# Signs of the weights by VectorE, three low bits by ScalarE, fewer TensorE transposes, and other durations in the planner

## The chip, the cores and the metric

The kernel runs on one core of a Trainium2 chip. The metric is device time in microseconds (us) of one execution; each version is timed in several runs and the median counts. One further execution is recorded by the hardware profiler. Engine names in the profile: PE is TensorE (PEld its weight loads), DVE is VectorE, ACT is ScalarE, POOL is GpSimd, SP is SyncE, whose queue (SPq) issues every DMA of this kernel.

## The reference

Clustered attention, followed by a two-layer MLP over its output:

```python
# q, k, v: [4, 8, 768, 64]; centroids: [8, 16, 64]
q_assign = argmax(einsum('bhsd,hcd->bhsc', q_n, c_n))      # rows normalised
k_assign = argmax(einsum('bhsd,hcd->bhsc', k_n, c_n))
scores = where(q_assign == k_assign, q @ k.T / 8, -1e9)
attn = exp(scores - max); attn = attn / (sum + 1e-9)
x = (attn @ v) as [3072, 512]
h = x @ w_in                                               # w_in [512, 2048]
g = s * relu(h) ** 2 + b
out = g @ w_out                                            # w_out [2048, 512]
```

q, k, v and centroids arrive as float32. The two weight matrices arrive as float64, so the kernel has to make float32 of them.

## The kernel before

**Attention.** There are 192 units, one for each batch, block of 128 query rows and head. A unit has its scores on PE (`sc`, two matmul pairs, one with the tiles KA and QA, one with KB and QB), a row maximum on DVE (`ssm<-sc`), an exponential on ACT (`p`), a transpose of `p`, and a product with V on PE (`px`), which DVE scales into `xs`. The first 16 units work in float32: PE transposes `p` (`turned`), ACT copies that out (`PT`), and `px<-vn,PT` is a float32 matmul. The later units split `p` into two float16 halves and let a DMA transpose them. Batch 0 has its K in four pairs of heads (hp 0 to 3: units 0 and 1, 2 and 3, and so on in each block) and its first two query blocks in two halves (hq 0 and 1). K and Q are split, transposed (KA, QA), compared with the centroids (`pk`, `pq`, the one-hot tiles `om`, `oe`, `oo`), and transposed once more with the one-hot part (KB, QB). `turn` does these transposes: with `early` set by PE in pieces of 8 blocks of 128x128, each piece copied out of PSUM by ACT (`KB<-turn`), else by a DMA transpose on SP's queue. Before the change all of batch 0's K and the Q of its first two query blocks are early.

**Weights.** 16 tiles of w_in and 16 of w_out, 128x512 each, are loaded alternately as raw float64 words into `wst` (512 KB each), and narrowed in the order `fetch`, `rebase`, `narrow`, `bound`. `rebase` (ACT) multiplies the high word, taken as float32, by 2^-112 into `w` and takes its sign into `wsg`, of which there are two buffers. `narrow` (DVE) shifts `w` left by three bits, by which the sign drops out, and puts the top three bits of the low word in. `bound` sums the absolute values by a matmul with ones (`pw` with a DVE maximum for w_in, `po`, one accumulating bank, for w_out); then POOL multiplies `w` by the sign. The tile `wst` lies in the pool `slot` of 19 buffers, which also holds the 16 pairs of narrowed weights. The MLP of the first two blocks (`h<-x,w`, `acc<-w,g`) works with these float32 weights; later, weights split into float16 (`ws`) are used.

**Order.** The kernel records each operation as a step; a planner (`Plan.order`) then goes through the steps with an estimated duration for each, gives every engine next what it can start first, and the instructions are emitted in that order. Each engine works through its own list in order. So a changed estimate changes no work, only the order of an engine's list. In the planner, DVE and POOL operations marked as shared push each other back.

Of the kernel before, what the change touches and what calls it, by code (L numbers as in the profile page):

```python
# [37 lines left out]
class Plan:  # L38


    LIGHT = 2.4
    SIGNAL = 40.0

    def __init__(self, tc):
        self.tc = tc
# [83 lines left out]
    def takes(self, step):  # L129

        method, args, kwargs = step.calls[0]
        aps = [a for a in args if isinstance(a, bass.AP)]
        if step.queue.name == "PE":
            total = 0.0
            for _, args, _ in step.calls:
                n = self.width(args[0])
                if args[1].dtype == F32:
                    total += max(n * 4 / self.LIGHT, 112.0)
                else:
                    total += 56.0 if n == P else max(n / self.LIGHT + 2.5, 26.0)  # L140
            return total, False
        n = max(self.width(a) for a in aps)
        banks = any(a.space == PSUM for a in aps)
        small = all(a.dtype in (F16, BF16) for a in aps[:2])
        name = step.queue.name
        if name == "DVE":
            if method in ("tensor_reduce", "reciprocal"):
                return 145 + n / 0.96, method == "reciprocal" and not banks
            if method == "tensor_tensor":
                return 148 + n / 0.96, not banks  # L150
            if method == "scalar_tensor_tensor":
                return (200.0 if n == 1 else 165 + n * 1.1), not banks
            fold = 1 if banks else 4 if small else 2
            return 150 + n / 0.96 / fold, not banks
        if name == "ACT":
            more = 110 if "accum_out" in kwargs else 0
            if banks:
                return (170 + n * 0.84 if small else 140 + n * 1.1 if n > 700 else 130 + n * 0.97) + more, False
            return (100 + n * 1.1 if args[2] == AF.Copy and "scale" in kwargs else 100 + n * 1.0) + more, False
        if method == "tensor_tensor":  # L160
            return 165 + n * 1.93, True
        if method == "tensor_copy":
            return 60 + n * 1.35, True
        return 100.0, True

    def transfer(self, step):
# [6 lines left out]
        n = self.width(ap) // P  # L173
        return (1300.0 if n < 12 else 1480.0), 1300.0, n * 165.0, 500.0

    def order(self):
        steps = self.steps
        after = [[] for _ in steps]
        open_ = [len(s.waits) for s in steps]
        for s in steps:  # L180
# [23 lines left out]
        while left:  # L204
            best = None
            for q, line in pending.items():
                now = clock[q]
                choice = None
                for k in line:
                    at, need = max(ready[k], now), {}  # L210
                    for t in steps[k].tiles:
                        if t.name in held:
                            continue
                        tag = self.tag(t)
                        if turn[t.name] != given[tag] + need.get(tag, 0) or len(spare[tag]) <= need.get(tag, 0):
                            at = None
                            break
                        at = max(at, spare[tag][need.get(tag, 0)])
                        need[tag] = need.get(tag, 0) + 1
                    if at is None:  # L220
                        continue
                    if q == "SP" and len(landed) >= 8:
                        at = max(at, landed[-8])
                    mine = (max(at, now + 30), self.weight[k], at, k)
                    if choice is None or mine < choice:
                        choice = mine
                if choice and (best is None or choice[2] < best[2]):
                    best = choice + (q,)
            _, _, at, k, q = best
            s = steps[k]  # L230
            pending[q].remove(k)
            for t in s.tiles:
                if t.name not in held:
                    held.add(t.name)
                    given[self.tag(t)] += 1
                    spare[self.tag(t)].pop(0)
            started[k] = at
            if q == "SP":
                issue, pre, work, post = self.transfer(s)
                begin = max(at + pre, engines_free)  # L240
                engines_free = begin + work
                clock[q] = at + issue
                end = begin + work + post
                landed.append(end)
            else:
                long, shared = self.takes(s)
                end = at + long
                if q == "DVE" and shared:
                    for a, z in pool[-6:]:
                        if a < at + 60 < z:  # L250
                            end = max(end, z + long - 118)
                    port.append((at + 60, end))
                if q == "POOL":
                    a = at
                    for x, z in port[-6:]:
                        if x < at + 60 < z:
                            a = max(a, z - 60)
                    end = a + long
                    pool.append((a, end))
                clock[q] = end - {"PE": 0, "DVE": 70, "POOL": 45, "ACT": 90}[q]  # L260
                end += 60 if q == "PE" else 0
            for j in after[k]:
                open_[j] -= 1
                same = steps[j].queue.name == q == "PE"
                ready[j] = max(ready[j], end - 60 if same else end + self.SIGNAL)
                if not open_[j]:
                    pending[steps[j].queue.name].append(j)
            for t in s.tiles:
                users[t.name] -= 1
                if not users[t.name]:  # L270
                    heapq.heappush(spare[self.tag(t)], end + self.SIGNAL)
                    spare[self.tag(t)].sort()
            left -= 1
# [19 lines left out]
def tile_cluster_attention_mlp(ctx, tc, q, k, v, cent, w_in, w_out, s_in, b_in, out):  # L293
# [159 lines left out]
    def rebase(d):  # L453
        hw = d["st"][:, :, :, 1].bitcast(F32)
        A.activation(d["w"], hw, AF.Copy, scale=2.0 ** -112)
        d["sg"] = sb.tile([P, KT, P], BF16, tag="wsg", name=f"wsg_{d['p']}", bufs=2)
        A.activation(d["sg"], hw, AF.Sign)

    def narrow(d):
        c = d["w"].bitcast(I32)  # L460
        V.tensor_scalar(c, c, 3, None, op0=ALU.logical_shift_left)
        V.scalar_tensor_tensor(c.bitcast(U32), d["st"][:, :, :, 0].bitcast(U32), 29, c.bitcast(U32),
                               op0=ALU.logical_shift_right, op1=ALU.bitwise_or)

    sums = {}

    def bound(d):
        w, p, ft = d["w"], d["p"], d["ft"]
        top = w.bitcast(BF16).rearrange("p a (f z) -> p a f z", z=2)[:, :, :, 1]
        if p % 2:  # L470
            g = int(ft >= EARLY)
            if ft in (0, EARLY):
                sums[g] = (ps_m if g else ps_a).tile([P, 512], F32, tag="m" if g else "acc", name=f"po_{g}")
            done = ft in (EARLY - 1, NF - 1)
            M.matmul(sums[g], ones, top, start=ft in (0, EARLY), stop=done)
            if done:
                V.tensor_reduce(glob[:, 8 + g : 9 + g], sums[g], axis=AX.X, op=ALU.max)
        else:
            pw = ps_m.tile([P, 512], F32, tag="m", name=f"pw_{ft}")
            for t in range(KT):  # L480
                M.matmul(pw[:, :P], ones, top[:, t, :], start=(t == 0), stop=(t == KT - 1))
            V.tensor_reduce(w1[:, ft : ft + 1], pw[:, :P], axis=AX.X, op=ALU.max)
        G.tensor_tensor(w, w, d["sg"], op=ALU.mult)
        if ft == NF - 1:
            (finish_w_out if p % 2 else finish_w_in)()

# [94 lines left out]
    def prep_k(b, hp):  # L581
# [25 lines left out]
        KA = sb.tile([P, 2 * T, P], F16, tag="KA", name=f"KA_{n}", bufs=5)  # L607
        KB = sb.tile([P, 2 * T, P], F16, tag="KB", name=f"KB_{n}", bufs=5)
        KS[(b, hp)] = (KA, KB)
        turn(KA, ka.rearrange("p h t e d -> p (h t e d)"), b == 0)  # L610
        yield
        yield
        pa = ps_m.tile([P, 512], F32, tag="m", name=f"pk_{n}")
# [6 lines left out]
                M.matmul(o, KA[:, i, :], cT[:, 1, hc], start=False, stop=True)  # L620
        mk = kb.rearrange("p h t e (r c) -> p (h t) e r c", c=C)[:, :, 1, :, :]
        yield from onehot(pa, 2 * T, f"k{n}", mk, BIG, -BIG)
        turn(KB, kb.rearrange("p h t e d -> p (h t e d)"), b == 0)

    def prep_q(b, c, hq):
        n = f"{b}_{c}_{hq}"
# [25 lines left out]
        QA = sb.tile([P, m, P], F16, tag="QA", name=f"QA_{n}", bufs=3)  # L652
        QB = sb.tile([P, m, P], F16, tag="QB", name=f"QB_{n}", bufs=3)
        QS[(b, c, hq)] = (QA, QB, sm)
        turn(QA, qa.rearrange("p n e d -> p (n e d)"), b + c == 0)
        yield
        yield
        pa = ps_m.tile([P, 512], F32, tag="m", name=f"pq_{n}")
# [6 lines left out]
                M.matmul(o, QA[:, i, :], cT[:, 2, hc], start=False, stop=True)  # L665
        mk = qb.rearrange("p n e (r c) -> p n e r c", c=C)[:, :, 1, :, :]
        yield from onehot(pa, m, f"q{n}", mk, BIG, 0.0)
        turn(QB, qb.rearrange("p n e d -> p (n e d)"), b + c == 0)


    VS = {}
# [411 lines left out]
```

## Time and profile before

| | |
|---|---|
| median of 3 runs | 943.94 us (939.25 to 948.49) |
| profiled execution | 945.36 us, span 943.7 us |
| busy, share of the span | PE 91%, DVE 68%, ACT 67%, POOL 55% |
| mean granted TensorE clock | 0.96 |

The span is the time from the first to the last instruction in the trace; the profiled execution's own time is 1.7 us above it. A row of the timeline has start, duration, engine, line, operation, output<-inputs with their shapes and a count, and in brackets the engine's idle time before it with what ended it. A row of groups has busy time and mean duration, then the idle time before them. A row of stages has, for each engine, its busy time and its instructions, then the granted TensorE clock, the DMA share and GB/s. All helpers record through one line, so nearly every instruction has the same line number, and rows are told apart by the names of tiles.

### The profile page before, as it was taken

What the parts mean: (1) busy time and instruction counts of PE and PEld (TensorE: products, weight loads), DVE (VectorE), ACT (ScalarE), POOL (GpSimd) and SP (SyncE); (2) the same over time, 40 slices, a digit from 0 to 9 for tenths busy, and PEclk for the clock granted to TensorE, in tenths of its full rate; (3) what the DMA queues carried; (4) which work ended last, traced back from release to release, by engine and by line L of the source; (5) the groups of instructions that cost most, each with busy time, mean ns of one, the idle gap of its engine ahead of it and who ended that gap; (6) DMA issues with size and microseconds to landing.
All of it is one profiled execution on the core that took longest, in us unless ns stands there. A gap on an engine that the chain in (4) does not pass through costs nothing. (4 is left out here: it accounts for less than half of the span.)

```text
span 943.7 us, 26567 instructions
## 1 busy us (share of the span) xinstructions
PE 860.8 (91%) x10885; PEld 644.1 (68%) x10885; DVE 642.9 (68%) x1704; ACT 628.8 (67%) x921; POOL 521.5 (55%) x443
## 2 busy tenths in 40 slices
PE   1659779999889999999989999999989999999997
PEld 1437568777656777777767677777667777777774
DVE  7897778679968777476769575577778664754410
ACT  5759645488746866757767667667568667587632
POOL 1125442346556666567656667576567666576521
PEclk9778759999999999999999999999999999999999
DMA  8525333569698998878999989799999898987620
GB/s 306 186 73 197 97 87 85 107 132 157 125 216 159 213 154 168 134 146 147 195 193 186 188 136 160 128 142 157 176 166 164 152 142 150 137 153 125 117 42 23
DMA packets 400683, 139.67 MB, mean 148 GB/s; under 512 B 386224, under 2 KB 386224, under 8 KB 400560
## 3 DMA queue, kind: packets, MB, share of 16 engines
q1 hardware_dynamic: 400560, 137.97, 77.6%
q8 instruction: 85, 1.39, 0.6%
q14 instruction: 38, 0.31, 0.1%
HBM read 35.69 MB, written 6.29 MB: 44 GB/s over the span
## 5 line engine op out<-in xcount | busy, mean ns | idle before, releaser
L289 POOL TENSOR_TENSOR ph<-p,ph 128x768 f16<-128x768 f32 x176 | 295.0, 1677 | 231.8 <-ACT ph L289 209.9
L289 PEld LDWEIGHTS <-ws 128*128 128x128 f16 x4224 | 252.1, 99 | 32.8 <-issue 5.1
L289 PE MATMUL h<-x,ws 128*128 128x128 f16 x4224 | 266.0, 220 | 2.5 <-DMA x<-xn 1.4
L289 PE MATMUL acc<-ws,g 128*128 128x512 f16 x1056 | 257.0, 380 | 7.2 <-POOL g L289 6.1
L289 DVE TENSOR_REDUCE ssm<-sc 128x1 f32<-128x768 f32 x192 | 183.0, 953 | 101.2 <-PE sc L289 100.6
L289 ACT ACTIVATE p<-sc,ssm,qsm 128x768 f32<-128x768 f32 x192 | 188.7, 983 | 91.3 <-DVE ssm L289 51.9
L289 PEld LDWEIGHTS <-g 128*128 128x128 f16 x1056 | 97.7, 98 | 105.4 <-POOL g L289 9.4
L289 ACT ACTIVATE ph<-p 128x768 f16<-128x768 f32 x176 | 146.9, 835 | 21.5 <-DMA PT<-ph 13.8
L289 POOL TENSOR_TENSOR g<-r,g 128x512 f16<-128x512 f32 x88 | 102.9, 1170 | 45.4 <-ACT r L289 33.3
L289 PE MATMUL px<-vh,PT 128*128 128x65 f16 x2112 | 113.5, 194 | 5.0 <-DMA PT<-ph 2.6
L289 PEld LDWEIGHTS <-PT 128*128 128x128 f16 x3168 | 107.2, 98 | 11.7 <-issue 3.6
L289 PE MATMUL sc<-KA,QA 128*128 128x384 f16 x384 | 96.6, 335 | 15.6 <-ACT p L289 15.4
L289 PE MATMUL px<-vl,PT 128*128 128x64 f16 x1056 | 107.3, 192 | 0.0
L289 PE MATMUL sc<-KB,QB 128*128 128x384 f16 x384 | 96.7, 335 | 0.5 <-ACT QB L289 0.5
L289 ACT ACTIVATE r<-h,cf 128x512 f32<-128x512 f32 x88 | 59.9, 680 | 43.7 <-PE h L289 31.5
L289 POOL TENSOR_TENSOR w<-w,wsg 128x512 f32<-128x512 f32 x32 | 40.0, 1261 | 70.5 <-PE pw L289 43.6
L289 PEld LDWEIGHTS <-QA 128*128 128x128 f16 x768 | 44.5, 99 | 40.0 <-issue 21.7
L289 DVE TENSOR_SCALAR ssm<-px 128x2 f32<-128x2 f32 x88 | 13.8, 157 | 80.2 <-PE px L289 79.5
L289 ACT ACTIVATE g<-r 128x512 f16<-128x512 f32 x88 | 55.1, 626 | 1.9
L289 ACT ACTIVATE r<-r 128x512 f32<-128x512 f32 x88 | 54.7, 622 | 1.3
L289 PEld LDWEIGHTS <-QB 128*128 128x128 f16 x384 | 37.2, 100 | 24.1 <-issue 1.9
L289 POOL TENSOR_TENSOR xn<-xs,xn 128x256 f16<-128x256 f32 x44 | 30.5, 693 | 32.5 <-ACT xn L289 26.8
(128 smaller groups left out, 1090.2 us busy)
## 6 DMA issues: line engine op xcount, KB each, us to landing
wst<-in_moe_w_in_dram SPq DMA_DIRECT2D x16, 512.0 KB, 4.7
wst<-in_moe_w_out_dram SPq DMA_DIRECT2D x16, 512.0 KB, 4.8
kn<-in_k_dram SPq DMA_DIRECT2D x16, 384.0 KB, 3.9
qn<-in_q_dram SPq DMA_DIRECT2D x24, 256.0 KB, 3.9
vn<-in_v_dram SPq DMA_DIRECT2D x16, 384.0 KB, 3.8
out_dram<-o SPq DMA_DIRECT2D x24, 256.0 KB, 2.4
PT<-ph SPq DMA_TRANSPOSE x176, 4.1
x<-xn SPq DMA_TRANSPOSE x44, 3.0
```

Of the source, the lines that this page charges most:

```text
L289: self.tc.keep_in_program_order(getattr(s.queue.engine, method)(*args, **kwargs))
```

## The change

The high word's sign goes into `w` on DVE, after the sum of absolute values: the POOL product and the tile `wsg` go. The low word's top three bits are made by ACT, in place in `wst`, as the integer part of a multiplication, so that one DVE operation shifts and joins, where there were a shift and a joining. `wst` is now read last by the sign's operation behind `bound`. PE transposes only hp 0 of batch 0's K, and hq 0 of the Q of its first two query blocks; the rest goes to DMA transposes. The planner gets other durations for float32 matmuls and transposes on PE, a PE that takes twice as long after a slack stretch of 3413 ns, and fewer DVE operations marked as shared.

```diff
     LIGHT = 2.4
     SIGNAL = 40.0
+    SPAN = 3413.0
+    ENOUGH = 0.38
...
                 if args[1].dtype == F32:
-                    total += max(n * 4 / self.LIGHT, 112.0)
+                    total += max(n * 2 / self.LIGHT, 111.0) * (1 if call == "transpose" else 2)
...
             if method in ("tensor_reduce", "reciprocal"):
-                return 145 + n / 0.96, method == "reciprocal" and not banks
+                return 145 + n / 0.96, False
...
+            if method == "tensor_scalar" and n == 1:
+                return 150.0, False
...
+    def stream(self, at, long):
+
+        while True:
+            k = int(at // self.SPAN)
+            rate = 1.0 if self.busy.get(k - 1, 0.0) >= self.ENOUGH * self.SPAN else 0.5
+            room = ((k + 1) * self.SPAN - at) * rate
+            if room >= long:
+                self.busy[k] = self.busy.get(k, 0.0) + long
+                return at + long / rate
+            self.busy[k] = self.busy.get(k, 0.0) + room
+            long -= room
+            at = (k + 1) * self.SPAN + 1e-6
...
+            elif q == "PE":
+                end = clock[q] = self.stream(at, self.takes(s)[0])
+                end += 60
...
         A.activation(d["w"], hw, AF.Copy, scale=2.0 ** -112)
-        d["sg"] = sb.tile([P, KT, P], BF16, tag="wsg", name=f"wsg_{d['p']}", bufs=2)
-        A.activation(d["sg"], hw, AF.Sign)
+        low = d["st"][:, :, :, 0]
+        A.activation(low, low.bitcast(U32), AF.Copy, scale=7.49 * 2.0 ** -32)

     def narrow(d):
-        c = d["w"].bitcast(I32)
-        V.tensor_scalar(c, c, 3, None, op0=ALU.logical_shift_left)
-        V.scalar_tensor_tensor(c.bitcast(U32), d["st"][:, :, :, 0].bitcast(U32), 29, c.bitcast(U32),
-                               op0=ALU.logical_shift_right, op1=ALU.bitwise_or)
+        bits = d["w"].bitcast(U32)
+        V.scalar_tensor_tensor(bits, bits, 3, d["st"][:, :, :, 0].bitcast(U32),
+                               op0=ALU.logical_shift_left, op1=ALU.bitwise_or)
...
-        G.tensor_tensor(w, w, d["sg"], op=ALU.mult)
+        V.scalar_tensor_tensor(w.bitcast(U32), d["st"][:, :, :, 1].bitcast(U32), 0x80000000, w.bitcast(U32),
+                               op0=ALU.bitwise_and, op1=ALU.bitwise_or)
...
-        turn(KA, ka.rearrange("p h t e d -> p (h t e d)"), b == 0)
+        turn(KA, ka.rearrange("p h t e d -> p (h t e d)"), b == 0 and hp < 1)
...
-        turn(QA, qa.rearrange("p n e d -> p (n e d)"), b + c == 0)
+        turn(QA, qa.rearrange("p n e d -> p (n e d)"), b + c == 0 and hq < 1)
```

KB and QB change as KA and QA do. The names below end in a running number that differs between the versions.

The first place is DVE's list, where the twelfth tile of w_in and that of w_out are narrowed (before: `w_309` with `wst_310` and `wst_315`; after: `w_274` with `wst_275` and `wst_279`), between the maximum of unit 11 and the scaling of units 6 and 7's product, which is `xs`. Before, beginning behind the second half of the tiles ahead:

```order
L289 TENSOR_SCALAR w_309<-w_309 128x512
L289 TENSOR_SCALAR vm_93<-vm_93 128x1
L289 SCALAR_TENSOR_TENSOR w_309<-wst_310,w_309 128x512
L289 TENSOR_SCALAR vm_93<-vm_93 128x1
L289 TENSOR_REDUCE ssm_282<-sc_326 128x1
L289 TENSOR_SCALAR vm_93<-vm_93 128x1 x2
L289 TENSOR_SCALAR ssm_282<-ssm_282,qsm_0_0_105 128x1
L289 TENSOR_REDUCE w_84<-pw_328 128x1
L289 TENSOR_SCALAR w_309<-w_309 128x512
L289 TENSOR_REDUCE qsm_1_1_339<-qn_1_1_322 128x8
L289 SCALAR_TENSOR_TENSOR w_309<-wst_315,w_309 128x512
L289 TENSOR_TENSOR xs_304<-px_334,ssm_230 128x128
```

After, from the same maximum of unit 11 on; `w_274<-wst_275,w_274` puts the signs in, `w_274<-w_274,wst_279` shifts and joins:

```order
L309 TENSOR_REDUCE ssm_250<-sc_288 128x1
L309 TENSOR_SCALAR vm_93<-vm_93 128x1 x2
L309 TENSOR_SCALAR ssm_250<-ssm_250,qsm_0_0_105 128x1
L309 TENSOR_REDUCE w_84<-pw_290 128x1
L309 SCALAR_TENSOR_TENSOR w_274<-wst_275,w_274 128x512
L309 SCALAR_TENSOR_TENSOR w_274<-w_274,wst_279 128x512
L309 TENSOR_SCALAR ssm_206<-ssm_206 128x2
L309 SCALAR_TENSOR_TENSOR vl_0_284<-vn_0_94,vm_93,vh_0_283 128x768
L309 RECIPROCAL ssm_206<-ssm_206 128x2
L309 TENSOR_REDUCE qsm_1_1_300<-qn_1_1_285 128x8
L309 TENSOR_TENSOR xs_269<-px_295,ssm_206 128x128
```

The tensor_scalar of a tile is gone, a scalar_tensor_tensor stands behind each maximum of `pw`, and the split of V, `vl`, has come ahead of `xs`.

The second place is SP's list in the same early part of the program, from the first load of V on. Before:

```order
L289 DMA vn_0_94<-in_v_dram 128x768
L289 DMA vn_1_95<-in_v_dram 128x768
L289 DMA wst_210<-in_moe_w_in_dram 128x1024
L289 DMA wst_221<-in_moe_w_out_dram 128x1024
L289 DMA wst_227<-in_moe_w_in_dram 128x1024
L289 DMA wst_233<-in_moe_w_out_dram 128x1024
L289 DMA vn_2_199<-in_v_dram 128x768
L289 DMA wst_239<-in_moe_w_in_dram 128x1024
L289 DMA wst_244<-in_moe_w_out_dram 128x1024
```

After, a little further down, from the third load of V on:

```order
L309 DMA vn_2_181<-in_v_dram 128x768
L309 DMA vn_3_182<-in_v_dram 128x768
L309 DMA wst_204<-in_moe_w_in_dram 128x1024
L309 DMA wst_209<-in_moe_w_out_dram 128x1024
L309 DMA wst_214<-in_moe_w_in_dram 128x1024
L309 DMA wst_218<-in_moe_w_out_dram 128x1024
L309 DMA_TRANSPOSE KB_1_118<-kb_1_111 128x12x128
L309 DMA wst_225<-in_moe_w_in_dram 128x1024
L309 DMA wst_229<-in_moe_w_out_dram 128x1024
L309 DMA_TRANSPOSE QB_0_1_153<-qb_0_1_149 128x8x128
L309 DMA_TRANSPOSE KB_2_151<-kb_2_145 128x12x128
L309 DMA wst_235<-in_moe_w_in_dram 128x1024
```

Eight transposes, of which three are seen here, now stand between the loads of the weights; a load behind one is issued only after it.

More of the change, by code (lines that the diff above doesn't have):

```diff
@@ L134, in takes @@
             total = 0.0
-            for _, args, _ in step.calls:
+            for call, args, _ in step.calls:
                 n = self.width(args[0])
                 if args[1].dtype == F32:
-                    total += max(n * 4 / self.LIGHT, 112.0)
+                    total += max(n * 2 / self.LIGHT, 111.0) * (1 if call == "transpose" else 2)
                 else:
@@ L174, in transfer @@
         return (1300.0 if n < 12 else 1480.0), 1300.0, n * 165.0, 500.0
+    def stream(self, at, long):
[9 more added lines that the diff above has]
+            at = (k + 1) * self.SPAN + 1e-6
     def order(self):
         steps = self.steps
+        self.busy = {}
         after = [[] for _ in steps]
@@ L259, in order @@
                     pool.append((a, end))
-                clock[q] = end - {"PE": 0, "DVE": 70, "POOL": 45, "ACT": 90}[q]
-                end += 60 if q == "PE" else 0
+                clock[q] = end - {"DVE": 70, "POOL": 45, "ACT": 90}[q]
             for j in after[k]:
@@ L622, in prep_k @@
         yield from onehot(pa, 2 * T, f"k{n}", mk, BIG, -BIG)
-        turn(KB, kb.rearrange("p h t e d -> p (h t e d)"), b == 0)
+        turn(KB, kb.rearrange("p h t e d -> p (h t e d)"), b == 0 and hp < 1)
     def prep_q(b, c, hq):
@@ L667, in prep_q @@
         yield from onehot(pa, m, f"q{n}", mk, BIG, 0.0)
-        turn(QB, qb.rearrange("p n e d -> p (n e d)"), b + c == 0)
+        turn(QB, qb.rearrange("p n e d -> p (n e d)"), b + c == 0 and hq < 1)
     VS = {}
```

## The prediction

> **What bounds the kernel now.** I read the busy shares and their slices first. Each digit is the busy share of one of 40 slices of 23.6 us.
>
> ```profile
> PE 860.8 (91%) x10885; PEld 644.1 (68%) x10885; DVE 642.9 (68%) x1704; ACT 628.8 (67%) x921; POOL 521.5 (55%) x443
> ...
> PE   1659779999889999999989999999989999999997
> ...
> DVE  7897778679968777476769575577778664754410
> ```
>
> TensorE is at 9 nearly everywhere from the seventh slice on, and at 1 to 9 in the first six. The change touches the weights, the K and Q of batch 0 and the planner, and the first two lie in those early slices. So I asked for the stages, cut at 14 us, where the first weight is narrowed, and at 146 us, where unit 16's score maximum starts and the last weight has been narrowed; the row of transposes alone (the `turn` tiles) has PE and ACT only.
>
> ```profile
> 14.00:146.00 132.00, 92.01 (x700) 72.25 (x700) 105.10 (x244) 91.08 (x162) 48.22 (x40) 0.77 0.43 143
> 146.00:250.00 104.00, 101.63 (x992) 76.97 (x991) 88.05 (x195) 74.84 (x109) 45.94 (x32) 0.98 0.63 120
> 14.00:146.00 132.00, 15.05 (x128) 16.34 (x20) 0.77 0.43 143
> ```
>
> The busy columns are PE, PEld, DVE, ACT, POOL. Up to 146 us VectorE is the busiest, 105.1 of 132 us, and TensorE idles 40 us at a granted clock of 0.77. From 146 us on TensorE is busy 101.6 of 104. So time saved in the early stage comes out of the end, since what follows is a filled TensorE whose work the change leaves alone; the early stage is set by VectorE's list, and 26.9 us of it are idle.
>
> ```profile
> L289 DVE SCALAR_TENSOR_TENSOR w<-wst,w 128x512 uint32<-128x512 uint32 x32 | 30.3, 950 | 0.0
> ...
> L289 DVE SCALAR_TENSOR_TENSOR vl<-vn,vm,vh 128x768 f16<-128x768 f32 x3 | 3.9, 1303 | 0.0
> ...
> L289 DVE TENSOR_SCALAR w<-w 128x512 int32<-128x512 int32 x32 | 17.7, 563 | 2.4 <-ACT w L289 2.4
> ...
> L289 DVE TENSOR_SCALAR qsm<-qsm 128x8 int32<-128x8 int32 x8 | 2.5, 311 | 0.0
> L289 DVE TENSOR_TENSOR qsm<-qsm,ksm 128x8 f32<-128x8 f32 x8 | 2.2, 279 | 0.0
> ```
>
> ```profile
> L289 POOL TENSOR_TENSOR w<-w,wsg 128x512 f32<-128x512 f32 x32 | 40.0, 1261 | 70.5 <-PE pw L289 43.6 <-PE po L289 7.6 <-ACT vh L289 5.3
> ```
>
> ```profile
> DVE xs L289 <- PE px L289: 15.8, 6, 4.4
> ...
> POOL w L289 <- PE pw L289: 43.6, 10, 11.6
> ...
> POOL w L289 <- PE po L289: 7.6, 3, 4.4
> ...
> DVE w L289 <- PE pw L289: 3.6, 6, 1.0
> ```
>
> These rows are VectorE's groups, GpSimd's product of weights and signs, and the waits, all of 14 to 146 us. Narrowing the weights takes 30.3 + 17.7 = 48.0 us, nearly half of VectorE's work; 15.8 us of its idle time is `xs` waiting for the float32 product `px`. The means hide two speeds, which the timeline shows:
>
> ```profile
> 13.99 0.43 DVE L289 TENSOR_SCALAR w<-w 128x512 int32<-128x512 int32 x1 [2.37 <-ACT w L289]
> ...
> 16.22 0.68 DVE L289 SCALAR_TENSOR_TENSOR w<-wst,w 128x512 uint32<-128x512 uint32 x1
> ...
> 45.93 1.42 DVE L289 SCALAR_TENSOR_TENSOR w<-wst,w 128x512 uint32<-128x512 uint32 x1
> ...
> 45.64 1.15 POOL L289 TENSOR_TENSOR w<-w,wsg 128x512 f32<-128x512 f32 x1 [11.62 <-PE pw L289]
> ```
>
> The same instruction takes 0.68 us alone, and 1.42 us while GpSimd's product runs from 45.64 to 46.79: it ends 0.56 us behind the product, as if held until then.
>
> **The change, part by part.** All sums are against the profiled execution, 945.4 us.
>
> *Weights on VectorE.* Before, alone, a tile costs 0.43 + 0.68 = 1.11 us. After, it costs two operations of the 0.68 form, 1.36 us: by bare work VectorE gets 32 x 0.25 = 8 us more. But 48.0 us is what it now pays, since GpSimd's products stretch it. With these gone, 64 x 0.68 = 43.5 us: **-4.5 us**. The new pair's operands lie otherwise than in the row (the strided `wst` second, or as high words). Bounds: all at the disturbed mean of 0.95 us make 60.8 us, +12.8; below, 64 at 0.66 us, the row's rounding and a little, -5.8. I take the undisturbed row, since without its product GpSimd keeps 8.2 of its 48.2 us in this stage.
>
> A rule speaks against this: the Trainium skill, in "Vector Engine (DVE) Microarchitecture Reference", section "Points that are easy to get wrong", says that a scalar_tensor_tensor with two SBUF sources that aren't bfloat16 runs at half throughput. This trace disagrees: 0.68 us for 512 elements of two uint32 sources, which is not half of the page's own 1.0417 ns for each element (section "Measured stream behaviour on trn2"), from which half rate would give 1.07 us, an estimate, and this term 20 us more instead of 4.5 less.
>
> *What else the product stretched.* Operations on VectorE beside it, with a lone instance of each:
>
> ```profile
> 7.44 0.16 DVE L289 TENSOR_SCALAR qsm<-qsm 128x8 int32<-128x8 int32 x1
> ...
> 18.99 0.15 DVE L289 TENSOR_TENSOR qsm<-qsm,ksm 128x8 f32<-128x8 f32 x1
> ...
> 141.53 0.99 DVE L289 SCALAR_TENSOR_TENSOR vl<-vn,vm,vh 128x768 f16<-128x768 f32 x1
> ```
>
> Against the means above: 8 x (0.311 - 0.16) + 8 x (0.279 - 0.15) + 3 x (1.303 - 0.99) = 1.2 + 1.0 + 0.9, **-3 us**. Bounds: 0, if GpSimd's remaining copies do it, and -5 with the smaller groups.
>
> *Order around `px`.* The planner counted a float32 matmul of 64 columns as 112 ns and will count 222; a pair of units' product has 12 of them.
>
> ```profile
> 77.09 2.79 PE L289 MATMUL px<-vn,PT 128*128 128x64 f32 x24
> ...
> 83.58 2.89 PE L289 MATMUL px<-vn,PT 128*128 128x64 f32 x24
> ...
> 92.02 4.57 PE L289 MATMUL px<-vn,PT 128*128 128x64 f32 x24 [0.35 <-DVE w L289]
> ...
> 106.12 4.98 PE L289 MATMUL px<-vn,PT 128*128 128x64 f32 x24 [0.66 <-DVE w L289]
> ...
> 128.57 5.22 PE L289 MATMUL px<-vn,PT 128*128 128x64 f32 x24
> ...
> 142.88 2.89 PE L289 MATMUL px<-vn,PT 128*128 128x64 f32 x24
> ```
>
> ```profile
> 111.14 0.29 DVE L289 TENSOR_TENSOR xs<-px,ssm 128x128 f32<-128x128 f32 x1 [3.24 <-PE px L289]
> ```
>
> Planned at 1.34 us, the product takes 2.8 to 5.2 us with the granted clock; so `xs` stood too early in VectorE's list and held everything behind it, here for 3.24 us. At this place the list before has between unit 11's maximum and `xs` one shift, one joining, a maximum over Q and five small ones, about 2.4 us at their lone durations; the list after has two of the 0.68 us form, `vl` at 0.99 and the same maximum over Q, about 4.0 us. So 1.6 us of the 3.24 are filled, half. Over all six waits I take half of 15.8: **-8 us**. Bounds: 0, where the work put ahead of `xs` is missed elsewhere, and -15.8.
>
> *New waits.* The sign's operation must come behind PE's sum of absolute values. For w_in it stands behind the maximum of `pw`, which waits already, 3.6 us over 16. For w_out it waits for `po` itself, 16 times. Queued behind it are VectorE's next narrowing and the next score maximum, for which ACT's exponential waits. I take as much again as for `pw`: **+3.6 us**. Bounds: 0, and the 7.6 us which GpSimd's product waits for `po` now.
>
> *ScalarE.* The sign becomes a copy in place with a strided integer output.
>
> ```profile
> L289 ACT ACTIVATE wsg<-wst 128x512 bf16<-128x512 f32 x32 | 21.4, 674 | 12.3 <-POOL w L289 12.3
> ...
> L289 ACT ACTIVATE KB<-turn 128x1024 f16<-128x1024 f16 x4 | 4.1, 1023 | 6.8 <-PE turn L289 6.8
> ```
>
> ```profile
> PE sc L289 <- ACT p L289: 9.2, 7, 2.5
> ...
> PE acc L289 <- POOL g L289: 6.1, 5, 3.4
> ```
>
> No row has such an output. Between 0.67 us, the row it replaces, and 1.02, the row with twice the elements (11 us more over 32), I take 0.67: nothing. It is hidden either way, by 132 - 91.1 = 41 us in which ScalarE idles; uncovered it is +11. The 12.3 us that the sign waited for GpSimd's free buffer go too; what is late next is VectorE.
>
> *Transposes.* PE loses 88 of its 128, 15.05 x 88/128 = 10.3 us, and ScalarE 14 of its 20 copies, 11 to 12 us. Both were beside a busier VectorE: nothing, though the 6.8 us wait of `KB` bounds the gain. In their stead SP issues eight DMA transposes:
>
> ```profile
> KB<-kb SPq DMA_TRANSPOSE x12, 5.1
> ```
>
> ```profile
> 58.82 1.44 PE L289 MATMUL turn<-ident,kb 128*128 128x128 f16 x12 [2.30 <-DVE kb L289]
> ```
>
> ```profile
> 59.87 1.51 ACT L289 ACTIVATE KB<-turn 128x1024 f16<-128x1024 f16 x2 [4.55 <-PE turn L289]
> ```
>
> ```profile
> 48.19 0.33 SPq L289 DMA_DIRECT2D wst<-in_moe_w_out_dram  x1
> 62.67 0.33 SPq L289 DMA_DIRECT2D wst<-in_moe_w_in_dram  x1
> ...
> 101.31 1.34 SPq L289 DMA_TRANSPOSE QA<-qa  x1
> ```
>
> Each takes 1.34 us of SP's queue and about 5 us to land. The queue has room (14.5 us between the two loads shown), and VectorE's other narrowing covers the landing: nothing. Uncovered, the three KB stand in series ahead of units 2, 4 and 6, each at 5.1 less the 2.6 us that a turn takes now (58.82 to 61.38), +7.5. Loads behind a transpose come later by its wait for `kb`; I cost that at nothing too, since they are 2 tiles each.
>
> *Later order.* The lists after 146 us differ in places of VectorE's, hardly of TensorE's. TensorE's largest waits after 150 us stand behind ScalarE's rows above; I take **0**, and for one such group gone or doubled +-6 us.
>
> Sum: -4.5 - 3 - 8 + 3.6 = **-12**, so 945.4 - 12 = 933.4 us for a profiled execution. The median shown, 943.9, lies 1.4 us under the profiled execution; the forecast for the median is **932 us**, -1.3%.
>
> **The rivals.**
>
> *Colder TensorE: no change.* With 88 transposes fewer, TensorE is slacker from 14 to 60 us, and a slack TensorE is granted a lower clock: 0.77 in this stage against 0.98 after it. If the three of six `px` that now run at about 2.8 us go at 5.0, and VectorE waits for each, +6.4 and the half of the waits not gained (+8) make a median of 946. With only one of the two, 938 to 940; within 1% either way. For it: the 4.57 to 5.22 us rows. Against it: the work that stays is packed into less time. The Trainium skill, "TensorE: Matmul & The Clock Gate", section "Part 1: The HAM clock gate", speaks for it: half clock after an idle window of some 3.4 us, full after a busy one. The two durations of `px` agree with that, and no run here yet shows the slack that the lost transposes leave.
>
> *VectorE inherits GpSimd's waits: slower.* GpSimd's product stood 51.2 us waiting for `pw` and `po` in 13 waits, and nobody was queued behind it. Now the sign is in VectorE's list, ahead of score maxima. Without the +3.6, the gain is 15.5 us, so from 15.5/32 = 0.5 us per sign the kernel is slower; at 1 us each, 945.4 - 15.5 + 32 = 962, a median of 960. Against it: the list shown has other work between the joining and its sign.
>
> *The half rate, or disturbed operations.* With 64 at 1.36 us in place of 43.5 us: 87 us, and +32 instead of -12 makes a median of 976. The 0.68 us row speaks against it.
>
> *More than expected.* All of the 15.8 us of waits, and the 6.8 us of `KB`, gone: -4.5 - 3 - 15.8 - 6.8 = -30, a median of 914.
>
> **How the numbers follow.** Forecast (922 to 937 us) 0.50; colder TensorE or waits that stay (937 to 950) 0.26; inherited waits 0.11; half rate 0.02; more than expected (907 to 922) 0.11. The median of the likeliest is 932. The range from 911 to 948 leaves out the slow rivals, 0.13, and the tails of the outer cases, some 0.05. About 1% is what a measurement of this kernel can tell: 9.4 us, so faster is below 934.5. Faster: the 0.11 and nearly 0.85 of the forecast's span, with the rest lying above it, 0.55. Same: 0.32. Slower: 0.13.
>
> **What would show it.** Right: `w<-wst,w` and its twin at about 0.68 us with no second speed; no GpSimd row of `w`; `xs` waits under 10 us; a stage up to unit 16's maximum that is about 12 us shorter, and from there on to the end the same 798 us. Wrong: a new wait of VectorE `w` for PE `po` or `pw` far over 7 us; `px` rows at 5 us throughout; SP's waits for `kb` ahead of the loads, with ACT `w` waiting for `wst`; or a longer stretch after unit 16.

## The result, and the profile after

The median is 929.57 us (928.25 to 932.31, 4 runs) beside 943.05 us for the kernel before: a ratio of 0.986, with a 95% interval of 0.982 to 0.990. It is faster by 1.4%, where 1.3% was forecast, and 2.4 us under the predicted 932. The number was right and its parts were not: the early stage gained more than twice what was forecast, and over a third of that lead was gone at the end. That two errors cancelled is luck.

The profiled execution took 928.25 us, its span 926.5. Unit 16's score maximum, the seventeenth `ssm<-sc` on VectorE's timeline, closes the early stage; here it is in the kernel before and in the changed one:

```profile
146.14 0.95 DVE L289 TENSOR_REDUCE ssm<-sc 128x1 f32<-128x768 f32 x1
```

```profile
118.40 0.95 DVE L309 TENSOR_REDUCE ssm<-sc 128x1 f32<-128x768 f32 x1
```

It comes 27.7 us earlier. I call that the lead at unit 16, and follow it through the program: the time of a unit's maximum before, less the same unit's time in the other kernel. The lead is 25.1 us at unit 48, 20.4 at unit 64 and 17.1 at the last unit, 191, which is the difference of the two spans. So 10.6 us of the lead went between unit 16 and the end.

The stage rows of the changed kernel, first from 14 us to unit 16, then the 104 us that were shown of before (busy time of PE, PEld, DVE, ACT, POOL, then granted clock, DMA share, GB/s):

```profile
14.00:118.40 104.40, 76.51 (x591) 59.13 (x590) 97.04 (x247) 80.41 (x149) 8.69 (x8) 0.85 0.70 206
```

```profile
146.00:250.00 104.00, 101.06 (x1115) 72.13 (x1114) 86.47 (x209) 73.35 (x107) 52.66 (x37) 1.00 0.77 142
```

VectorE's busy time in the stage fell from 105.1 to 97.0 us, its idle time from 26.9 to 104.4 - 97.0 = 7.4 us. GpSimd kept 8.7 us, and TensorE was granted 0.85 of its clock instead of 0.77. VectorE's groups in the stage, and its waits (us in total, times, longest):

```profile
L309 DVE SCALAR_TENSOR_TENSOR w<-w,wst 128x512 uint32<-128x512 uint32 x32 | 22.1, 695 | 3.5 <-ACT wst L309 3.5
L309 DVE SCALAR_TENSOR_TENSOR w<-wst,w 128x512 uint32<-128x512 uint32 x32 | 21.7, 685 | 0.4 <-PE po L309 0.2
...
L309 DVE SCALAR_TENSOR_TENSOR vl<-vn,vm,vh 128x768 f16<-128x768 f32 x4 | 4.0, 1008 | 0.0
...
L309 DVE TENSOR_TENSOR qsm<-qsm,ksm 128x8 f32<-128x8 f32 x8 | 2.8, 349 | 0.0
```

```profile
DVE w L309 <- ACT wst L309: 3.5, 1, 3.5
DVE w L309 <- PE pw L309: 2.6, 2, 1.7
DVE xs L309 <- PE px L309: 1.7, 3, 1.1
...
DVE w L309 <- PE po L309: 0.2, 1, 0.2
```

Both forms of the weights' operation ran at one speed, 0.69 us, and the two waits that the prediction reckoned with, for `px` and for `po`, are all but gone. ScalarE's in-place copy, for which before had no row, cost what the sign had cost:

```profile
L309 ACT ACTIVATE wst<-wst 128x512 int32<-128x512 uint32 x32 | 21.4, 669 | 4.9 <-DMA wst<-in_moe_w_in_dram 2.6 <-DMA wst<-in_moe_w_out_dram 2.3
```

From 150 us on, two of TensorE's waits grew. Before and after:

```profile
PE acc L289 <- POOL g L289: 6.1, 5, 3.4
...
PE pq L289 <- DMA QA<-qa: 1.8, 4, 0.7
```

```profile
PE pq L309 <- DMA QA<-qa: 12.6, 12, 2.1
PE acc L309 <- POOL g L309: 9.4, 9, 2.5
```

### The profile page after: what moved, and what is told of

It reads as the page before. It is cut to its first block, busy times and chain, and to the rows that moved or that the text cites. A ratio compares the mean times of both kernels' runs of the same rounds, so it can differ in the third digit from the quotient of the medians.

```text
span 926.5 us, 26346 instructions
## 1 busy us (share of the span) xinstructions
PE 849.6 (92%) x10797; PEld 629.4 (68%) x10797; DVE 630.0 (68%) x1704; ACT 619.4 (67%) x907; POOL 483.6 (52%) x411
## 4 chain that ended last, share of the span: by engine, by line
PE 30%; DMA 8%; DVE 5%; issue 5%; POOL 4%; ACT 1%; SPq 0%; POOLq 0%; ACTq 0%; DVEq 0%
PE h L309 11%; PE acc L309 11%; PE sc L309 4%; DMA QA<-qa 4%; PE px L309 4%; POOL qa L309 2%; DVE ssm L309 1%; DMA qn<-in_q_dram 1%; POOL ph L309 1%; DMA PT<-ph 1%; POOL g L309 1%; DVE qsm L309 1%; ACT ph L309 1%; PE pq L309 1%; DMA KB<-kb 1%
## 5 line engine op out<-in xcount | busy, mean ns | idle before, releaser
L309 PE MATMUL acc<-ws,g 128*128 128x512 f16 x1056 | 260.5, 382 | 9.9 <-POOL g L309 9.4
L309 ACT ACTIVATE ph<-p 128x768 f16<-128x768 f32 x176 | 147.0, 835 | 29.5 <-DMA PT<-ph 17.2
L309 PE MATMUL px<-vh,PT 128*128 128x65 f16 x2112 | 110.8, 193 | 0.6 <-DVE xs L309 0.6
L309 PE MATMUL sc<-KA,QA 128*128 128x384 f16 x384 | 96.3, 333 | 11.9 <-ACT p L309 10.6
L309 PEld LDWEIGHTS <-PT 128*128 128x128 f16 x3168 | 104.9, 97 | 3.3 <-issue 1.5
L309 PE MATMUL px<-vl,PT 128*128 128x64 f16 x1056 | 105.4, 191 | 0.0
L309 PEld LDWEIGHTS <-QA 128*128 128x128 f16 x768 | 41.3, 98 | 45.6 <-DMA QA<-qa 19.0
L309 POOL TENSOR_TENSOR qa<-qn,qb 128x512 f16<-128x512 f32 x22 | 26.5, 1204 | 72.3 <-ACT qb L309 71.9
L309 POOL TENSOR_TENSOR xn<-xs,xn 128x256 f16<-128x256 f32 x44 | 30.9, 701 | 25.2 <-ACT xn L309 22.5
```

The costliest lines, as they stand in the source:

```text
L309: self.tc.keep_in_program_order(getattr(s.queue.engine, method)(*args, **kwargs))
```

## The experiments

The change has three parts that can be had apart: W, the weights (`rebase`, `narrow`, `bound`); T, the fewer turns; P, the planner's durations. P has three pieces: the float32 costs; `stream`, the slower PE after a slack stretch; and the marking as shared. In all runs the planner makes the order anew, and none of them leaves work out. Ratios are against the kernel before, timed beside it on the same chip. VectorE's busy and idle time and the leads are those of one profiled execution each, and all leads are taken against the one of the kernel before.

| run | parts | ratio (95% interval) | VectorE busy / idle, 14 us to unit 16 | lead at unit 16 / at the end |
|---|---|---|---|---|
| the change | W, T, P | 0.986 (0.982 to 0.990) | 97.0 / 7.4 | 27.7 / 17.1 |
| w_only | W | 0.992 (0.989 to 0.995) | 96.0 / 24.3 | 11.8 / 10.0 |
| t_only | T | 0.998 (0.995 to 1.001) | 104.7 / 23.9 | 3.6 / 0.6 |
| p_only | P | 0.995 (0.991 to 0.998) | 104.4 / 18.7 | 9.0 / 4.5 |
| w_and_t | W, T | 0.982 (0.977 to 0.987) | 95.2 / 19.5 | 17.5 / 19.0 |
| w_and_p | W, P | 0.988 (0.984 to 0.991) | 97.9 / 15.9 | 18.3 / 17.7 |
| no_shared | W, T, P less the marking | 0.986 (0.984 to 0.988) | 97.5 / 7.4 | 27.2 / 16.2 |
| no_stream | W, T, P less `stream` | 0.991 (0.986 to 0.996) | 94.9 / 8.9 | 28.3 / 14.9 |
| w_t_f32 | W, T, float32 costs | 0.982 (0.978 to 0.986) | 95.6 / 15.3 | 21.2 / 21.7 |
| after_again | W, T, P | 0.989 (0.986 to 0.992) | 97.2 / 10.7 | 24.2 / 13.3 |
| w_t_f32_again | W, T, float32 costs | 0.974 (0.970 to 0.977) | 95.1 / 11.8 | 25.2 / 23.2 |

The two kernels that were run twice show how far a lead can be trusted: between two profiled executions of one kernel it differs by 3.5 and 4.0 us at unit 16, and by 3.8 and 1.5 us at the end. Smaller differences mean nothing here. The two ratios of W, T and the float32 costs, 0.982 and 0.974, come from two chips, and their intervals just miss each other; so ratios are compared below only where the runs stood beside each other, unless the text says otherwise. The stage does not hold quite the same work in every run either: in W alone, in W and T, without `stream` and with the float32 costs alone, some small operations, worth 3 us of VectorE by their durations, come only behind unit 16; the change has 1 us more work in the stage than the kernel before.

In the tests below the first fence is the stage's row from 14 us to the maximum of unit 16 (columns as above), the second holds rows of VectorE's waits in the same stretch, where nothing else is said.

**W alone.** The three functions as in the diff, nothing else.

```diff
-        G.tensor_tensor(w, w, d["sg"], op=ALU.mult)
+        V.scalar_tensor_tensor(w.bitcast(U32), d["st"][:, :, :, 1].bitcast(U32), 0x80000000, w.bitcast(U32),
+                               op0=ALU.bitwise_and, op1=ALU.bitwise_or)
```

> The weights' part alone (ACT's in-place copy, DVE's joining and sign, no GpSimd product); all of K and Q still turned by TensorE, planner as before. By the prediction's terms: DVE's work on the weights 48.0 to about 43.5 us, stretched neighbours -3, new waits +3.6, so about 4 us faster than before (939). Rival, that the idle time of VectorE went because GpSimd's product left the chain of buffers (wsg, its two buffers): 12 us or more faster (931 or less), with VectorE's idle time from 14 us to unit 16's maximum near 10 us. Other rival, that with 8 us more bare work on VectorE and the old order it gains nothing: 943.

Measured: 935.4 us beside 945.3, ratio 0.992. Its stage, and VectorE's waits in it:

```profile
14.00:134.32 120.32, 82.16 (x676) 65.29 (x676) 95.99 (x234) 91.77 (x163) 7.90 (x8) 0.83 0.47 157
```

```profile
DVE xs L289 <- PE px L289: 8.4, 5, 5.5
DVE w L289 <- PE pw L289: 4.7, 5, 2.0
...
DVE w L289 <- PE po L289: 2.5, 2, 1.3
```

VectorE's busy time fell by 9.1 us, of which 3 are the small operations that moved, against 7.5 forecast for both terms of GpSimd's product. Here the forecast new waits are real: `po` 2.5 us and `pw` 1.1 more. But `px` went from 15.8 to 8.4 us with the planner's durations untouched, by 7.4 us, nearly the 8 that the prediction expected of the new order with the new durations. The first rival, VectorE's idle time near 10 us, isn't borne out (24.3), nor is the second, no gain.

**T alone.** KA, QA and QB change as KB does.

```diff
-        turn(KB, kb.rearrange("p h t e d -> p (h t e d)"), b == 0)
+        turn(KB, kb.rearrange("p h t e d -> p (h t e d)"), b == 0 and hp < 1)
```

> Fewer turns by TensorE alone; weights and planner as before. By the prediction's terms: no change (943, within 2 us), since VectorE stays the longer list. Rival, read off the two traces, where unit 4's maximum comes 12.2 us earlier: the turns held units 4 to 7 up, and this part alone gives 8 to 12 us (931 to 935).

Measured: 943.4 beside 945.3, ratio 0.998, no change by its interval. The prediction's zero held: unit 4 came 10.1 us early, as the rival had it, but unit 10 was 11.0 us late. The stretch between, from 60 to 105 us, first in the kernel before, then with T alone, and VectorE's longest wait with T alone:

```profile
60.00:105.00 45.00, 35.65 (x263) 28.17 (x261) 34.97 (x77) 37.10 (x73) 25.80 (x21) 0.82 0.45 138
```

```profile
60.00:105.00 45.00, 34.48 (x166) 27.73 (x166) 33.93 (x68) 24.66 (x49) 17.82 (x15) 0.64 0.37 107
```

```profile
DVE xs L289 <- PE px L289: 8.6, 3, 3.5
```

TensorE had a granted clock of 0.64 there, where it was 0.82 before, and GpSimd still had its products (17.8 us busy). VectorE idled 11.1 of the 45 us, 8.6 of them waiting for `px`; before it idled 10.0, 5.6 for `px`. From 14 to 105 us VectorE worked 74.3 us with T alone and 75.8 before. So its list was no further on, although unit 4 had come early.

**P alone.**

```diff
-                    total += max(n * 4 / self.LIGHT, 112.0)
+                    total += max(n * 2 / self.LIGHT, 111.0) * (1 if call == "transpose" else 2)
```

This edit, `stream` and the marking, as in the change's diff.

> The planner's durations alone; the same operations as before in another order. By the prediction's terms: VectorE's wait for px falls by about 8 us and so does the time (935). Rival: the new durations order the early stage better (15 us or more), and give some 10 us back after unit 48, where the changed kernel's lead falls from 25 to 17 us with TensorE's pq waiting 12.6 us for QA's transpose: then this run shows such waits, too, and a net of 5 to 8 us (935 to 938). Third: no effect, 943.

Measured: 939.0 beside 945.3, ratio 0.995.

```profile
14.00:137.17 123.17, 83.35 (x690) 65.48 (x690) 104.43 (x251) 91.09 (x163) 46.33 (x40) 0.79 0.45 151
```

```profile
DVE w L309 <- PE pw L309: 10.0, 11, 2.0
DVE xs L309 <- PE px L309: 2.9, 2, 1.9
```

The term as the prediction put it is right in kind: `xs` waits 2.9 us instead of 15.8. Two thirds of that were kept: the wait for `pw` grew from 3.6 to 10.0 us, so VectorE's idle time fell by 8.2 us, the -8 forecast. Half of this lead of 9.0 us was lost by the end (4.5), with 6.1 us of `pq` waits.

**W and T.**

> Weights and turns with the planner as before, the changed kernel without its planner's part. If the parts add up as the prediction has them: 4 us faster (939). If the planner's part costs the 8 to 10 us that are given back late, this run keeps its early lead: lead at unit 16 and at the end alike, and about as fast as the changed kernel or faster (920 to 930), with pq waiting for QA's transposes 2 us. If the planner's part is what takes VectorE's idle time away: 935 or more, and VectorE waiting for px some 15 us.

Measured: 925.7 beside 945.3, ratio 0.982; lead 17.5 us at unit 16 and 19.0 at the end.

```profile
14.00:128.67 114.67, 83.29 (x593) 63.62 (x593) 95.22 (x236) 80.64 (x149) 8.55 (x8) 0.79 0.66 189
```

```profile
DVE xs L289 <- PE px L289: 7.2, 2, 4.6
```

VectorE has no less to do than in W alone (95.2 us), but idles 19.5 us instead of 24.3; the waits for `px` stay near those of W alone. The lead is kept to the end, as the second expectation had it.

The fewer turns, worth nothing alone, add 5.7 us at unit 16 and 9 us at the end to W. And the kernel without P is as fast as the whole change, by intervals of two series that overlap.

**W and P.**

> Weights and the planner's durations, all turns left on TensorE. If each part brings its own in the early stage (weights 11.8, planner 9.0 us of lead at unit 16): lead 18 to 21 us there, and with a late loss like the changed kernel's 930 to 935. If the turns are what the changed kernel's early lead needs, as the lead of 12 us at unit 4 in both kernels with fewer turns suggests: lead 12 us or less at unit 16, 935 or more.

Measured: 932.9 beside 944.7, ratio 0.988; lead 18.3 at unit 16, 17.7 at the end, as its first expectation had it. Unit 4 is 3.9 us late in it, where the change has it 12.2 us early; the lead of W and P is made behind unit 10. So the early lead at unit 4 is T's, in all runs. But T added no time to W and P: the whole change, run beside it (`after_again`), took 933.9 us. Its lead at unit 16 was 5.9 us larger, and at the end 4.4 us smaller.

**P without the marking; P without `stream`.** Each takes one piece out of the change (of the second, the place where `stream` is used):

```diff
-                return 145 + n / 0.96, False
+                return 145 + n / 0.96, method == "reciprocal" and not banks
...
-            if method == "tensor_scalar" and n == 1:
-                return 150.0, False
```

```diff
-            elif q == "PE":
-                end = clock[q] = self.stream(at, self.takes(s)[0])
-                end += 60
```

> The changed kernel without one part of the planner's: DVE's reciprocals and one-column operations stay marked as shared, as before. If this marking is what costs the late 8 to 10 us (it holds for all of the program, and the float32 costs only for its first two blocks): early lead at unit 16 near 27 us, kept to the end, so 917 to 922. If the late loss has another source, some chance of order: 926 to 932 with a loss of 8 us or more between unit 16 and the end.

> The changed kernel without the planner's slower PE after a slack stretch (stream); the float32 costs and the marking stay. If stream is what places work well in the early stage: lead at unit 16 falls to 18 to 22 us, and the late loss stays, so 933 to 938. If the float32 costs do it: lead at unit 16 stays near 27 us, 929.

Measured: 927.1 (0.986) and 932.3 (0.991) beside 940.2. Both keep the early lead (27.2 and 28.3), and both lose 11 and 13 us of it later. So neither piece alone is needed for the early lead, nor for the late loss; the expectation that the marking does it was wrong.

**W, T and the float32 costs alone.**

> Weights, turns and only the float32 costs of the planner. If these costs alone take VectorE's waits for px away, as the prediction had it: xs waits under 3 us (7.2 us without them), lead at unit 16 near 27 us and kept, 917 to 922. If they don't matter beside weights and turns: as without any of the planner's part, 926, lead 17 us.

Measured: 923.6 beside 940.2 (0.982), and again 919.6 beside 944.7 (0.974). VectorE's wait for `px` in the early stage, and TensorE's largest waits from 150 us on:

```profile
DVE xs L289 <- PE px L289: 6.6, 4, 3.8
```

```profile
PE sc L289 <- ACT p L289: 9.0, 8, 2.4
...
PE pq L289 <- DMA QA<-qa: 2.5, 4, 1.0
```

The `px` waits didn't fall under 3 us, where they were expected (6.6, and 4.2 the second time), but the lead of 21 to 25 us is kept to the end within 2 us (21.7, 23.2).

**GpSimd products beside the changed kernel.** 32 products of the old size on a tile that nothing reads, each behind the maximum of a w_in tile:

```diff
+        G.tensor_tensor(idle, idle, w1[:, ft : ft + 1].unsqueeze(2).broadcast_to([P, KT, P]), op=ALU.mult)
         V.scalar_tensor_tensor(w.bitcast(U32), d["st"][:, :, :, 1].bitcast(U32), 0x80000000, w.bitcast(U32),
```

> The changed kernel with 32 GpSimd products of 128x512 float32 added again in the early stage, on a tile that nothing reads. The prediction's term: what GpSimd's product stretches on VectorE is worth 4.5 us plus the 8 us of bare work, so the operations on weights go from 0.69 back to 0.85 us or more in the mean, VectorE's busy time up to unit 16 grows by 8 to 13 us, and the kernel is 5 to 12 us slower than the changed one (935 to 941). Rival: VectorE isn't held by a product outside its chain, the means stay at 0.69, 930.

Measured: 953.4 beside 940.2, ratio 1.014 (1.010 to 1.017): 24 us over the change's median, 26 by the two ratios, where 5 to 12 were expected. Its stage up to unit 16, the weights' forms in it, and the products (up to 160 us):

```profile
14.00:140.28 126.28, 84.62 (x590) 66.69 (x590) 113.04 (x241) 82.07 (x149) 51.45 (x40) 0.80 0.59 172
```

```profile
L309 DVE SCALAR_TENSOR_TENSOR w<-w,wst 128x512 uint32<-128x512 uint32 x32 | 32.4, 1015 | 4.1 <-ACT wst L309 4.1
L309 DVE SCALAR_TENSOR_TENSOR w<-wst,w 128x512 uint32<-128x512 uint32 x31 | 23.1, 745 | 0.9 <-PE po L309 0.6
```

```profile
L309 POOL TENSOR_TENSOR idle<-idle,w 128x512 f32<-128x512 f32 x32 | 43.0, 1344 | 66.2 <-DVE w L309 43.1 <-DVE ssm L309 22.0
```

Nothing waits for these products, and yet VectorE's busy time grew from 97.0 to 113.0 us and its idle time from 7.4 to 13.2. The lead at unit 16 fell from 27.7 to 5.9. The stretching of VectorE is shown, and its price is 16 us of VectorE's work, above the upper end expected. The rest of the 24 us isn't attributed: the planner pushes such products and VectorE's operations apart, so the order differs too, and the late loss is in this run as well (lead -10.3 at the end).

**A later place for `pq`.** The changed kernel, with more for the landing of a DMA transpose in the planner:

```diff
-        return (1300.0 if n < 12 else 1480.0), 1300.0, n * 165.0, 500.0
+        return (1300.0 if n < 12 else 1480.0), 1300.0, n * 165.0, 1300.0
```

> The changed kernel with 0.8 us added to the planner's estimate of a DMA transpose's landing, so that TensorE's pq stands later in its list. If the late loss is pq waiting for QA's transpose (12.6 us in the changed kernel, 1.8 before): these waits fall under 4 us, the lead of 27 us at unit 16 is kept within 4 us to the end, 919 to 922. If the waits for pq only show a loss made elsewhere: they fall and the loss stays or moves to other rows, 926 to 932.

Measured: 934.6 beside 944.7, ratio 0.989 (0.984 to 0.993); lead 28.0 at unit 16, 18.0 at the end. TensorE's waits from 150 us on:

```profile
PE pq L309 <- DMA QA<-qa: 10.3, 9, 3.2
PE acc L309 <- POOL g L309: 8.8, 10, 1.9
```

The waits barely fell, and the loss stayed. The run didn't take the wait away that it was to test, so it settles nothing on it.

**The change and the better version side by side.**

> The changed kernel once more, beside the others on the same chip: 0.986 of the kernel before, as measured (0.982 to 0.990).

> Weights, turns and only the float32 costs once more, beside the changed kernel: if it is the better version, its interval against the kernel before lies below the changed kernel's (0.980 against 0.986); if the first result was chance, both are at 0.984.

Measured on one chip: the change 0.989 (0.986 to 0.992), W, T and the float32 costs 0.974 (0.970 to 0.977). The intervals are apart; medians 933.9 and 919.6 us. This version beats both kernels.

## Why the prediction was right, and where not

**VectorE's weights: right.** Forecast 64 x 0.68 = 43.5 us, measured 22.1 + 21.7 = 43.8. The rival of half rate would have shown 1.36 us; 0.69 it was. So the Trainium skill's halving rule (in "Vector Engine (DVE) Microarchitecture Reference", section "Points that are easy to get wrong") doesn't hold for these two uint32 sources on this chip.

**What the product stretched: right.** 105.1 - 97.0 = 8.1 us of VectorE's work went, against 4.5 + 3 forecast; 4.2 of them are the weights (48.0 to 43.8). The single rows chosen for the 3 us were partly wrong: `qsm<-qsm,ksm` has 349 ns now, more than the 279 before, while `vl` fell to 1008. That GpSimd's products stretch VectorE's work is shown by the run with products beside; which rows they stretch is not foreseen from a mean over a stage.

**Order around `px`: right in kind, its cause too narrow.** Forecast -8, measured 15.8 to 1.7 us, -14. P alone takes it to 2.9, but W alone to 8.4 without any of the new durations, and W, T and the float32 costs leave 6.6. The half taken from one place of the list was a guess at a sum of six.

**New waits: wrong for the change.** +3.6 was forecast; the waits for `po` and `pw` together are 2.8 us, less than the 3.6 of `pw` before. A wait for ScalarE's in-place copy, 3.5 us, once, stands in the place of one for ScalarE's `w`, 2.4 us. In W alone they did come, `po` 2.5 and `pw` 4.7. The rival of inherited waits had no place.

**Transposes: wrong.** They were costed at nothing because VectorE's list was longer. Alone that is so (0.998). With W it isn't: 0.992 against 0.982. The step that failed is taking each part's worth against the old list: there T's early units brought VectorE no further, and in the list without GpSimd's product they do. Whether by VectorE's shorter list or by the clock (0.73 in W and T from 60 to 105 us, 0.64 in T alone) was not separated. With W and P in place T brought nothing again, since the late loss came with it.

**Later order: wrong.** Forecast 0, +-6; measured +10.6 us, +10.9 in the second execution. Early stage: forecast -12, measured -27.7. The two errors, 15.7 and 10.6, cancel but for 5.1 us. It is by luck that the total lies so near the forecast: with the early stage as measured and the later one as forecast, the median would have been about 916 us (945.4 - 27.7 - 1.4).

**Colder TensorE: no, for the stage.** Its granted clock rose from 0.77 to 0.85. Rows of `px` on TensorE's timeline at two speeds stand side by side, as before:

```profile
65.43 2.89 PE L309 MATMUL px<-vn,PT 128*128 128x64 f32 x24
77.68 5.38 PE L309 MATMUL px<-vn,PT 128*128 128x64 f32 x24 [0.92 <-DVE w L309]
```

The rival showed in a part of the stage only: between 60 and 105 us the clock was 0.82 before, 0.64 in T alone, 0.73 in W and T and 0.77 in the change. Between 14 and 60 us, where the prediction had looked for it, it rose from 0.80 to 0.96 in T alone and in the change.

**What stays open** is the late loss. The rows from unit 16's maximum to the end, of the kernel before and of the changed one:

```profile
146.14:943.60 797.46, 767.85 (x10183) 571.28 (x10181) 530.22 (x1429) 534.03 (x754) 470.82 (x371) 0.99 0.84 147
```

```profile
118.40:926.50 808.10, 772.27 (x10205) 569.81 (x10203) 525.43 (x1428) 535.47 (x755) 472.35 (x371) 0.99 0.83 145
```

The changed kernel takes 10.6 us longer from there: TensorE is busy 4.4 us more and idle 6.2 us more, at the same clock. A part of it is work that has only changed sides, since one float32 product more, 22 recorded matmuls or 2.7 us, stands behind unit 16 in it:

```profile
L289 PE MATMUL px<-vn,PT 128*128 128x64 f32 x48 | 5.6, 273 | 0.0
```

```profile
L309 PE MATMUL px<-vn,PT 128*128 128x64 f32 x70 | 8.3, 273 | 0.0
```

Nor does the lead shrink evenly. In the change it is 27.4 us at unit 96, the first of batch 2, 18.4 at unit 112, 24.1 at unit 144, the first of batch 3, and 17.1 at the end; in P alone it is 17.2 at unit 144 and 4.5 at the end; in W and T it stays between 15 and 19. So in kernels with P the lead at a unit also shows where the planner has put that unit, by 8 us and more, and the 10.6 us aren't all lost time.

TensorE's idle time behind unit 16 is the surer sign. It is 29.6 us before and 35.8 in the change, and 34.9 to 36.5 in its second execution and in each variant of it that has T and also `stream` or the marking; these reach unit 16 with 24 to 28 us and the end with 13 to 18. It is 27.9 to 29.2 us in W and T, without or with the float32 costs, which keep their lead of 17.5 to 25 us within 2 us; 29.2 in W and P without T, which keeps its 18.3; and 28.8, 32.1 and 30.2 in W, T and P alone. The waits that grew, `pq` behind QA's transpose and `acc` behind GpSimd's `g`, aren't enough of a cause: without the marking they are 6.2 and 4.2 us, and the loss is 11 all the same; in W and P they are 6.9 and 7.4 us, and there is no loss. What the runs with W show is that the loss comes where T stands together with `stream` or the marking. Through which rows it comes was not settled; taking either piece away left the loss, and the run that was to move `pq` didn't.

## What to carry to other kernels

Price an operation at its lone duration and also at its duration beside the neighbour that the trace shows to hold it up: by lone durations VectorE's weights went from 32 x 0.43 + 32 x 0.68 = 35.5 us to 43.5, and yet VectorE was busy 8 us less. Parts of a change that are worth nothing against the old longest list can be worth something together: W and T brought 1.8%, W 0.8%, T nothing. And a planner's new estimates do not add to the rest: P alone gained 0.5%, but of its three pieces the float32 costs alone, with W and T, gave a kernel 1.5% faster (919.6 to 933.9 us) than all three.

## What was not expected of the hardware

GpSimd products that nothing waits for cost VectorE 16 us in 126 (113.0 against 97.0 us busy), and the kernel 24. They stretched mostly the shift and join (`w<-w,wst`, 695 to 1015 ns) and the sign's operation (`w<-wst,w`) little (685 to 745 ns), though both read the strided `wst`. What counted was which of the two engines began first, for instance here:

```profile
60.25 0.68 DVE L309 SCALAR_TENSOR_TENSOR w<-wst,w 128x512 uint32<-128x512 uint32 x1
60.85 1.52 DVE L309 SCALAR_TENSOR_TENSOR w<-w,wst 128x512 uint32<-128x512 uint32 x1
```

```profile
60.35 1.47 POOL L309 TENSOR_TENSOR idle<-idle,w 128x512 f32<-128x512 f32 x1 [1.42 <-DVE ssm L309]
```

The sign's operation began 0.10 us ahead of the product and took 0.68 us. The shift and join began within the product and ended 0.55 us behind it. In this run all 13 operations on the weights that began 0.1 to 0.25 us ahead of a product took 0.67 to 0.68 us; of the 17 that began with over 0.5 us of a product still to run, 15 ended 0.55 us behind its end. And a VectorE operation that reads every second 32-bit word was as fast as one on contiguous words (685 to 695 ns; 684 ns for `qn<-qn,qsm` of the same size), as was ScalarE's copy that writes every second word (669 against 670 ns).
